# An RWKV-7 scan with a SwiGLU block on one core: the copies of chunks 6 to 23 go from VectorE to ScalarE, in a new order of steps

## The chip, the cores and the metric

The kernel runs on one core of one Trainium2 chip. The metric is the time of one execution in device microseconds (us); of several runs the median counts. In the profile PE is TensorE (PEld its weight loads), DVE VectorE, ACT ScalarE, POOL GpSimd and SP the sync engine, which here only issues DMAs.

## The reference, cut to what matters

```
# attention: batch 4, heads 8, sequence 768, head_dim 40
for t in range(S):
    y[:, :, t] = einsum('bhd,bhde->bhe', rt, state)
    Sa = einsum('bhde,bhe->bhd', state, at)
    state_decay = state * wt[:, :, None, :] - einsum('bhd,bhe->bhde', Sa, bt)
    state = state_decay + einsum('bhd,bhe->bhde', vt, kt)
# then x = y as (3072 tokens, 320), d_ff = 1536
xn = x / sqrt(mean(x * x, -1) + 1e-6) * rms_g
g = xn @ w_gate
out = (g * sigmoid(g) * (xn @ w_val)) @ w_out
```

The 32 pairs of batch and head each carry a 40 x 40 state through 768 steps. Their outputs, eight heads side by side, are the 3072 tokens of the feed-forward block. All is in fp32; the three weight matrices arrive as 64-bit floats and are narrowed on the chip.

## The kernel before, in words

The sequence is cut into 24 chunks of 32 steps. A chunk is solved as a small triangular system, so that the state is only touched once a chunk. There are five stages, each of them a function that adds steps to a plan:

- `narrow(f, part)`, 24 times: loads one half of a slice of the weights, turns its 64-bit words into fp32 with three ACT and three DVE steps, and writes it to a DRAM buffer `sW`.
- `front(c)`, one a chunk: loads w, a, k, b and v (tiles `wan`, `kbn`, `VU`, `wn`), turns them on PE, and builds by levels of 1, 2, 4, 8 and 16 the decay products `T`, the scaled keys `K`, the matrices `Ab` and `aP`, the keys `KN` and the triangular matrix `LT`, which goes by DRAM (`sB`) into `M`.
- `inverse(c)` (`early_inverse` for chunks 0 to 3): inverts that matrix row by row on DVE, with one product (`tmp`) and one difference (`Yi`, or `M` in the early form) a row, and sends it by DRAM (`sY`) back into `LT`.
- `main(c)`, one a chunk: computes U on PE from the old state, copies it into `VU`, updates the state `ST`, forms the scores, multiplies them into five masked tiles `As`, gets the output `y` level by level, and turns y into tokens: the sum of squares on ACT, a power on POOL, the scaling `x`, and its transpose scaled by the norm's weights (`gcol`) into `xg`.
- `feed(g)`, one for two chunks: for each pair of the twelve weight slices the gate and value products (`h64` and `h`, into PSUM), `sg` = silu on ACT, `hT` = value times `sg` on DVE, and the output product into `po` (line 547, as all of `mm`).

Each step goes through a helper with a line of its own, so the profile shows the helper's line: L505 for all DVE steps, L525 `act`, L528 `copy` and L531 `scale` on ACT, L534 to L540 POOL, L544 DMAs, L547 `mm`, L550 `flip` (a transpose), and L1079 the warm matmul.

No loop sets the order of the work. `plan.issue(ORDER, PAIRS)` walks through a list of some 6000 words written into the file: each number picks one of the steps not yet issued, counted from the first that is left, and each engine runs its own steps in the order in which they come. A "-" issues a warm matmul of `ident` by `ident` into columns of PSUM that nobody reads. `PAIRS` says which of three pairs of PSUM banks each of the 499 temporary PSUM tiles ("rooms") takes. A step may wait for the step before it on its engine, for its inputs, and for the earlier user of its PSUM pair or of its buffer, of which there are one to three for each tile.

Two constants choose forms by chunk: `EARLY` (4) the form of the inverse, `LATE` (6) the engine of four kinds of step in `main`:

```
for i, q in each_iq:                                              # line 892, four copies of U a chunk
    (copy if c < LATE else dcopy if q else copy)(VU[...], U[...])
for i in range(2):                                                # line 912, even chunks
    (copy if c < LATE else dcopy)(R["r2"][half(i)], ps[half(1 - i), i])
if G == 1 and c < LATE:                                           # line 929, the top mask
    for i in range(2):
        scale(As[:, j, :, i], sc..., msi[:, j, i, 0:1])
elif G == 1 or l == 1:
    tt(As[:, j], sc..., msi[:, j:j + 1]..., MUL)
if c < LATE:                                                      # line 997, the norm's weights
    for kt in range(KT): scale(xt[:, :, kt], ps[:, :, kt], gcol[:, kt:kt + 1])
else:
    tt(xt, ps, gcol..., MUL)
```

`copy` and `scale` are ACT steps, `dcopy` and `tt` DVE steps. `KT` is 3. In `each_iq` half of the four entries have q = 1.

Of the kernel before, what the change touches and what calls it, by code (L numbers as in the profile page):

```python
# [22 lines left out]
EARLY, LATE = 4, 6  # L23
# [10 lines left out]
4 5 6 7 8 9 10 11 - - 46 - - - - 43 53 18 - 316 323 58 - - 61 47 60 525 27 44 - - - - 12 13 14 15 16 17 19 317  # L34
- - 313 315 324 314 333 327 328 - 318 325 - 326 - - 73 339 - 74 85 93 84 - 94 82 83 334 337 - 336 335 338 -
340 349 20 21 22 350 355 23 342 343 24 25 26 - 367 - 354 348 - 352 - 344 345 363 346 365 347 - - 351 75 76 362
353 360 628 397 29 - 443 455 - 452 442 36 32 56 - 48 38 59 54 31 441 35 456 - 636 - 451 444 - 62 453 446 33 -
454 - 37 70 45 - 626 445 - 41 638 356 125 122 - 1 332 331 321 103 322 113 114 329 - 95 86 98 379 359 78 79 364
87 361 374 366 - 376 - 378 - - - - 373 77 357 368 371 377 375 387 372 89 88 358 - 461 - 386 369 383 90 80 -
380 381 465 370 466 384 - - 99 463 464 462 470 341 - 91 471 - - 478 - - 481 482 - 385 467 395 468 477 - - 476  # L40
- 483 493 480 - 389 391 390 - - 104 392 81 394 393 105 123 102 472 490 479 627 633 64 42 50 398 448 34 - 623 -
57 67 624 55 - 459 49 634 460 449 52 65 457 51 635 637 - - 473 - 474 491 - 475 450 - - 625 96 492 - 97 396 494
- - 489 - 504 382 100 487 488 - 484 506 - - 399 400 495 401 - 402 403 503 404 - - - 485 496 405 406 407 500
408 409 - 410 505 - 411 - 412 413 414 415 416 507 417 418 497 419 516 420 421 643 422 423 424 - 499 425 426
427 428 - 106 644 - - 502 501 498 107 108 429 124 320 0 317 90 576 - 132 577 - 328 99 643 645 511 510 - 484 -
113 646 644 509 107 - - - - 506 - 507 - 512 658 - 386 650 651 - 663 467 675 - - - 108 116 - 109 662 428 647
516 517 518 515 131 - 521 114 648 124 522 - 657 508 - - - 652 429 578 567 524 - - 61 870 456 861 860 - 640 66
445 430 69 - 598 871 26 - 28 64 639 630 67 629 110 519 520 434 656 - 653 - 654 661 - 117 660 659 127 128 - 655
580 - 115 - - 674 - - 579 513 664 - - - 432 143 431 433 118 525 526 670 568 125 126 669 133 581 666 134 135
435 436 437 438 569 141 142 140 119 687 129 - 668 673 667 161 152 151 163 - 665 144 527 528 529 136 137 138  # L50
679 530 531 532 533 671 534 535 536 537 147 676 160 130 573 571 572 570 672 682 145 146 684 148 538 680 539
540 541 542 543 544 545 546 547 548 149 549 550 685 551 552 553 - 554 582 583 686 - 574 153 555 575 681 156
677 162 139 801 164 678 586 688 167 157 689 - 589 595 590 - 604 693 154 165 155 690 587 588 596 1 0 962 135
145 144 113 146 134 663 519 661 662 560 136 137 143 612 121 122 660 556 557 555 646 554 712 520 664 665 562
129 138 655 147 148 149 563 131 564 568 565 132 569 - 713 566 832 668 33 - 827 841 826 825 - - 837 521 - 835
669 842 828 836 838 0 830 524 522 523 165 521 164 714 656 658 569 138 653 713 669 670 671 - 672 570 673 149
674 571 - 572 675 676 677 678 525 842 526 847 846 843 845 844 - 848 527 153 154 132 162 665 528 715 163 962
139 679 680 150 140 174 141 681 151 682 859 683 684 685 851 849 858 666 852 863 686 687 688 853 717 719 716
718 155 166 156 857 861 689 854 864 690 855 158 691 860 159 856 169 876 157 - 160 850 862 - 692 - 869 722 720
723 - - 546 764 182 - 152 183 185 173 167 547 726 573 168 875 574 - 721 - 575 729 731 865 1009 1008 - 600 -  # L60
1019 599 1018 1016 576 866 693 888 730 735 867 738 737 694 734 732 193 161 184 577 657 175 727 578 728 736 874
695 696 697 868 698 699 871 - 870 739 186 963 733 170 171 - 966 964 - 176 965 177 - 187 873 188 746 745 178
179 740 952 741 742 743 744 - 877 883 879 882 700 194 - - 579 881 880 747 180 872 887 886 172 195 885 580 748
582 - 878 889 891 581 884 749 750 751 752 753 829 590 589 1010 1020 896 754 892 - 890 1026 1013 1027 205 701
202 203 1021 1012 - 1022 - 1023 702 828 1028 705 703 950 951 755 - - 1011 894 893 838 756 1017 0 725 726 576
15 851 850 577 848 772 16 852 849 855 864 17 714 8 - 9 10 18 856 857 578 580 867 - 869 581 525 1093 579 19 23
33 719 720 32 853 723 854 868 862 863 877 866 879 523 717 0 573 515 575 516 713 869 517 847 707 710 711 574 42
0 509 5 839 840 845 841 707 861 567 753 850 14 754 855 856 755 893 568 708 709 569 570 757 853 710 - 711 8 17
851 712 713 714 715 716 717 718 854 719 871 523 21 23 22 867 852 858 756 - 872 - 766 868 524 - 866 869 873 720
# [4 lines left out]
776 876 877 878 18 879 880 881 882 883 884 885 748 - - 871 749 872 - - 1073 944 945 1078 1077 1075 1076 1074  # L74
23 560 719 561 1079 720 562 563 5 6 7 1082 1083 8 - 1090 886 887 1095 1093 1106 1080 947 564 0 12 715 24 - 712
556 13 16 1080 714 23 713 0 878 879 880 0 0 1072 875 1068 709 550 1069 1075 1070 876 1078 1087 877 710 10 1085
11 18 0 1073 1081 1080 9 875 1068 548 549 - - 708 - 1077 709 - 1085 1083 1079 - 929 758 759 876 1086 0 926
1077 17 1087 549 550 22 992 0 15 14 1193 12 542 543 544 765 1239 764 1250 1033 775 1043 867 868 869 1052 750
870 1090 871 872 1082 751 1240 920 1085 752 923 1089 1099 873 1083 874 875 876 1088 9 877 878 879 922 1084 921
545 1079 926 546 880 881 882 0 1085 1079 15 5 18 926 882 0 15 16 5 1079 545 546 1089 928 - 547 - - 548 - - -  # L80
939 1090 882 883 884 8 885 886 887 888 889 890 930 1093 1085 751 1091 929 1094 941 549 551 550 552 937 935 936
18 931 1092 19 891 932 553 938 940 892 893 894 895 896 897 933 898 899 900 942 554 555 1099 1098 1100 9 1101
972 - 0 1170 1083 1084 1085 0 196 546 - 0 0 385 343 344 551 - 386 - 345 552 376 346 - - 387 349 347 415 348
350 354 353 352 351 364 365 390 - 196 195 548 388 549 197 389 553 - 537 554 555 556 557 558 559 560 561 562
563 391 392 393 394 395 - 564 565 566 567 568 569 570 571 572 573 574 575 576 577 396 273 634 637 636 635 0 0
0 0 - 617 393 394 - 0 0 0 615 691 676 463 675 686 680 690 674 687 682 685 684 677 474 571 572 573 574 575 392
576 577 578 579 580 581 582 583 584 585 586 587 588 589 590 591 592 593 464 393 394 395 617 361 362 692 698
396 695 694 - 696 697 693 - - - 398 397 399 758 701 702 712 - 618 400 401 402 616 709 714 594 595 596 597 699
# [1023 lines left out]
```

## Time and profile before

| | |
|---|---|
| median of 3 runs | 1048.17 us (1045.47 to 1050.28) |
| span of the profiled execution | 1035.9 us |
| time around that span | not given by the page; median less span is 12.3 us |
| busy PE / DVE / ACT / POOL | 989.6 / 832.1 / 450.8 / 309.1 us |
| warm matmuls (L1079) | 522 records, 92.5 us of PE |
| chain that ended last | PE 54%, DVE 30%, issue 5%, DMA 5%, ACT 3% |

A group's row names line, engine, operation, output and input tile, shapes and count, then busy us and mean ns of one, then the idle time of the engine just before and what ended it. A row of the stretches gives from and to, the length, then for PE, PEld, DVE, ACT and POOL the busy us and the number of instructions, then the granted TensorE clock, the DMA share and GB/s. A row of the chain gives start, length and work. One warm matmul makes two records, as each fp32 matmul here does.

### The profile page before, as it was taken

How to read it: one execution, taken by the hardware profiler on the slowest of the kernel's cores; microseconds unless marked ns; L12 is line 12 of the kernel's file. 1: busy time of each engine (PE TensorE's matmuls, PEld its weight loads, DVE VectorE, ACT ScalarE, POOL GpSimd, SP SyncE). 2: the span in 40 equal slices, each digit the busy share in tenths (PEclk: the TensorE clock that was granted, in tenths of full speed). 3: DMA queues.
4: the chain of work that ended last, by engine and by line, in shares of the span. 5: the costliest groups of instructions: out<-in, count | busy, mean ns of one | idle time of the engine just before them, and what ended most of it. 6: DMA issues, size and time to landing. Idle time of an engine off the chain costs nothing.

```text
span 1035.9 us, 56007 instructions
## 1 busy us (share of the span) xinstructions
PE 989.6 (96%) x24842; PEld 807.6 (78%) x24842; DVE 832.1 (80%) x2789; ACT 450.8 (44%) x1019; POOL 309.1 (30%) x554
## 2 busy tenths in 40 slices
PE   7987999999999999999999999999999999999998
PEld 7976877788887787787877787887787877778876
DVE  8987688686869899899989888888799898788410
ACT  5784775543553443443443433452434444341210
POOL 9633413041442233232244232333232432210000
PEclk9976699999999999999999999998999999999999
DMA  8877356755442634434443535334633624422222
GB/s 161 158 194 171 97 158 165 202 131 127 105 87 64 145 79 103 120 65 106 101 98 83 143 75 125 87 68 99 133 62 68 162 65 107 114 51 54 89 77 65
DMA packets 163538, 113.03 MB, mean 109 GB/s; under 512 B 124512, under 2 KB 142880, under 8 KB 163296
## 3 DMA queue, kind: packets, MB, share of 16 engines
q1 hardware_dynamic: 144928, 86.48, 33.8%
q0 software_dynamic: 16192, 22.64, 11.3%
q8 instruction: 195, 3.19, 1.3%
q10 hardware_dynamic: 2176, 0.33, 0.3%
q14 instruction: 47, 0.39, 0.1%
HBM read 93.39 MB, written 15.99 MB: 106 GB/s over the span
## 4 chain that ended last, share of the span: by engine, by line
PE 54%; DVE 30%; issue 5%; DMA 5%; ACT 3%; SPq 2%; POOL 1%; DVEq 0%; ACTq 0%; POOLq 0%
PE ps L547 36%; PE po L547 10%; DVE tmp L505 5%; DVE Yi L505 5%; PE ps L550 5%; DVE LT L505 4%; PE po L1079 3%; DVE K L505 3%; DVE As L505 2%; SPq L544 2%; DVE Ab L505 1%; DVE hT L505 1%; DMA wf<-sW 1%; DVE y L505 1%; DVE T L505 1%
## 5 line engine op out<-in xcount | busy, mean ns | idle before, releaser
L547 PE MATMUL ps<-xg,wf 128*128 128x256 f32 (+1 forms) x1728 | 353.8, 391 | 1.1 <-DMA wf<-sW 0.7
L547 PEld LDWEIGHTS ps<-xg,wf 128*128 128x128 f32 (+1 forms) x1728 | 263.1, 190 | 50.6 <-issue 15.2
L547 PE MATMUL po<-wf,hT 128*128 128x320 f32 x576 | 177.0, 445 | 0.1
L505 DVE TENSOR_TENSOR tmp<-Yi,M 128x60 f32<-128x60 f32 (+24 forms) x620 | 130.3, 210 | 19.8 <-DMA M<-sB 5.4
L505 DVE TENSOR_TENSOR Yi<-Yi,tmp 128x60 f32<-128x60 f32 (+24 forms) x620 | 129.8, 209 | 14.6
L525 ACT ACTIVATE sg<-ps 128x512 f32<-128x512 f32 x72 | 43.0, 597 | 216.5 <-PE ps L547 216.3
L547 PEld LDWEIGHTS po<-wf,hT 128*128 128x128 f32 x576 | 104.6, 191 | 37.0 <-issue 2.1
L544 POOL DMA_DIRECT2D kbn<-in_b_dram x92 | 53.8, 587 | 191.7 <-PE ps L547 169.9
L528 ACT COPY KN<-ps 128x640 f32<-128x640 f32 x96 | 66.3, 692 | 88.0 <-DVE LT L505 50.5
L505 DVE TENSOR_TENSOR K<-K,T 128x512 f32<-128x512 f32 (+1 forms) x192 | 94.0, 496 | 3.4 <-ACT K L528 2.7
L1079 PE MATMUL po<-ident 128*128 128x128 f32 x522 | 92.5, 313 | 3.3 <-DVE po L579 3.3
L505 DVE TENSOR_TENSOR hT<-ps,sg 128x512 f32<-128x512 f32 x72 | 49.6, 689 | 51.6 <-ACT sg L525 51.0
L528 ACT COPY K<-K 128x256 f32<-128x256 f32 (+1 forms) x168 | 72.6, 444 | 35.2 <-DVE K L505 25.0
L547 PEld LDWEIGHTS ps<-Ab,K 40*60 40x60 f32 (+2 forms) x4608 | 68.7, 129 | 19.7 <-issue 6.5
L505 DVE TENSOR_TENSOR As<-ps,msi 128x256 f32<-128x256 f32 (+1 forms) x186 | 82.9, 478 | 1.1 <-PE ps L547 0.6
L547 PE MATMUL ps<-Ab,K 40*60 40x56 f32 (+2 forms) x4608 | 78.2, 217 | 5.2 <-DVE K L505 2.5
L1079 PEld LDWEIGHTS po<-ident 128*128 128x128 f32 x522 | 73.9, 208 | 11.5 <-POOL wan L540 3.3
L544 POOL DMA_DIRECT2D VU<-in_v_dram x92 | 53.8, 586 | 93.5 <-PE ps L550 55.9
L547 PEld LDWEIGHTS ps<-As,KN 128*40 128x40 f32 x3072 | 68.1, 128 | 13.9 <-issue 8.4
L544 POOL DMA_DIRECT2D wn<-in_w_dram x92 | 51.9, 566 | 90.0 <-DVE KN L505 56.4
L547 PE MATMUL ps<-As,KN 128*40 128x32 f32 x3072 | 74.0, 208 | 3.7 <-issue 1.5
L544 POOL DMA_DIRECT2D kbn<-in_k_dram x92 | 53.4, 583 | 76.7 <-PE ps L547 73.3
(137 smaller groups left out, 1470.3 us busy)
## 6 DMA issues: line engine op xcount, KB each, us to landing
wf<-sW SPq DMA_DIRECT2D x82, 480.0 KB, 4.4
M<-sB SPq DMA_DIRECT2D x80, 128.0 KB, 3.6
rn<-in_r_dram SPq DMA_DIRECT2D x24, 160.0 KB, 5.0
out_dram<-o SPq DMA_DIRECT2D x48, 80.0 KB, 3.2
kbn<-in_b_dram POOLq DMA_DIRECT2D x92, 40.0 KB, 3.1
kbn<-in_k_dram POOLq DMA_DIRECT2D x92, 40.0 KB, 3.2
wan<-in_a_dram POOLq DMA_DIRECT2D x46, 80.0 KB, 3.7
wan<-in_w_dram POOLq DMA_DIRECT2D x46, 80.0 KB, 4.3
```

Of the source, the lines that this page charges most:

```text
L505: plan.add("DVE", kind, lambda at: fn(at(o), *m(at)), [o], aps(*args))
L525: plan.add("ACT", "act", lambda at: nc.scalar.activation(at(o), at(a), f, **kw), [o] + aps(acc), [a])
L528: plan.add("ACT", "copy", lambda at: nc.scalar.copy(at(o), at(a)), [o], [a])
L544: plan.add(by, "dma", lambda at: queue.dma_start(out=o, in_=i), [o], [i])
L547: return o, lhsT, rhs, lambda at: nc.tensor.matmul(at(o), lhsT, rhs, start=start, stop=stop, skip_group_check=True)
L550: return o, i, ident, lambda at: nc.tensor.transpose(at(o), i, ident)
L1079: plan.warm = lambda: nc.tensor.matmul(po_[:, 0, DM:DM + P], ident, ident, start=False, stop=False, skip_group_check=True)
```

## The change

`LATE` becomes 24, so all 24 chunks take the branch that chunks 0 to 5 took: in chunks 6 to 23 ACT makes all four copies of U instead of two, the two half copies of r in even chunks, the top mask as two scalings instead of one DVE product, and the norm's scaling as three scalings instead of one DVE product. The numbers of `ORDER` and `PAIRS` are new throughout; the old list has 6131 words with 261 "-", the new one 5949 with 25. Nothing else differs.

```diff
-EARLY, LATE = 4, 6
+EARLY, LATE = 4, 24
...
 ORDER = """
-4 5 6 7 8 9 10 11 - - 46 - - - - 43 53 18 - 316 323 58 - - 61 47 60 525 27 44 - - - - 12 13 14 15 16 17 19 317
...
+4 325 314 5 6 44 317 7 323 8 69 328 9 324 43 10 313 11 58 12 83 13 454 73 45 627 74 445 85 47 94 456 93 628 113 397
+333 318 458 326 337 14 15 16 334 18 75 350 355 367 48 17 441 316 338 19 637 20 78 327 76 336 23 335 442 315 114 27
...
```

More of the change, by code (lines that the diff above doesn't have):

```diff
@@ L39 @@
[L39 to L68, printed above, removed]
@@ L78 @@
[L78 to L87, printed above, removed]
@@ L208 @@
-573 574 638 562 217 417 418 703 699 694 692 704 702 695 705 693 709 494 419 - 420 732 575 576 577 578 579 731
-744 - 0 0 216 - 561 419 420 421 422 740 716 578 579 754 714 646 715 647 430 719 431 432 723 580 649 648 724
[34 rows of a table removed]
-574 575 576 577 578 579 580 581 582 583 584 585 - 586 587 588 589 590 591 592 593 594 433 595 596 597 638 598
[8 rows of a table removed]
[5 rows of a table added]
+368 636 386 107 384 461 383 108 398 369 385 462 91 380 465 370 623 464 463 109 92 54 381 390 634 391 638 392 - 68
[3 rows of a table added]
+408 - 484 502 65 28 492 506 42 70 49 803 500 582 600 525 409 487 153 52 41 132 32 504 410 411 66 72 165 499 412 413
[7 rows of a table added]
@@ new lines @@
+686 203 549 550 693 551 552 553 588 554 176 555 677 688 595 628 678 556 174 604 - - 175 689 590 699 177 698 592 863
+697 594 593 864 700 591 0 836 552 520 550 828 147 560 838 653 150 835 141 156 664 600 559 665 0 0 373 414 689 375 0
+414 373 676 415 416 0 415 23 0 372 690 560 416 449 561 498 494 563 5 6 502 417 - 15 0 417 372 517 15 22 6 418 518
+696 7 31 0 511 411 25 8 0 688 411 689 23 511 8 512 495 681 513 412 514 684 21 413 414 683 364 365 0 677 506 507 508
+0 672 675 508 356 4 357 856 0 844 508 374 854 4 21 6 509 510 22 5 404 405 30 543 0 838 297 0 503 838 23 671 504 0
@@ new lines @@
+504 366 535 538 671 505 678 506 484 683 536 507 537 0 667 27 0 822 27 535 17 18 670 502 503 0 503 670 1 2 - 0 817
+501 502 503 504 505 532 663 - 506 507 4 508 509 0 534 663 474 545 31 521 0 382 680 532 28 660 531 664 383 384 665
[3 rows of a table added]
+741 17 493 30 0 664 0 543 666 542 541 0 0 658 607 665 23 815 666 807 808 657 32 14 685 - 544 671 809 668 811 669 6
+1053 672 810 670 546 24 15 674 545 812 824 829 486 547 0 809 480 2 15 541 810 666 735 10 670 821 9 11 0 803 734 733
+831 539 540 735 478 721 0 828 667 478 803 8 492 493 669 668 671 675 670 676 722 842 724 677 678 679 680 681 - 682
[6 rows of a table added]
@@ new lines @@
+540 840 1047 1055 766 700 0 0 1052 537 837 840 697 1036 15 1048 913 914 841 1237 - 1049 538 916 539 1050 843 844
[7 rows of a table added]
+484 640 331 332 333 334 529 541 335 0 334 335 336 337 338 339 471 340 341 342 369 0 - 1110 342 343 344 537 551 369
+621 552 635 622 388 715 345 346 347 349 553 636 348 392 393 - 554 394 624 194 197 350 555 395 196 699 195 396 556
[37 rows of a table added]
+389 678 666 958 0 436 - 660 971 959 - 969 960 769 608 609 775 774 662 777 659 437 961 668 958 661 970 432 438 610
[24 rows of a table added]
+869 881 826 870 880 876 1173 868 827 702 861 456 464 862 828 873 871 877 467 872 691 874 964 - 692 694 882 883 829
[6 rows of a table added]
@@ new lines @@
+771 596 597 598 599 642 644 600 744 601 602 643 756 - 959 437 741 745 757 436 603 640 604 605 606 755 1 740 761 556
+749 760 758 - 754 977 - 645 607 1127 608 646 751 752 763 609 610 764 753 - 774 611 612 772 766 433 765 613 438 655
+439 614 615 389 616 617 618 619 620 621 647 656 659 390 670 775 622 623 968 773 672 449 1126 778 434 777 440 769
+759 776 666 767 663 - 648 441 779 713 497 442 660 662 661 459 855 624 625 626 958 668 458 667 665 671 703 664 679
[3 rows of a table added]
+451 452 985 993 989 636 994 857 861 997 860 859 996 858 - 1174 453 1173 807 808 809 810 990 811 864 454 865 1007
[13 rows of a table added]
@@ new lines @@
+672 459 - 673 759 770 - 661 660 762 771 769 855 631 713 458 671 669 674 675 676 677 678 679 963 1 962 680 960 783
+784 681 977 785 786 787 447 767 973 788 633 853 452 448 766 854 789 682 454 634 790 791 792 793 794 795 683 970 856
+796 684 636 797 685 798 455 799 800 801 802 803 804 805 961 978 983 972 806 780 979 982 971 980 987 807 981 988 781
+808 809 456 986 810 811 812 813 814 - 984 985 815 686 687 688 816 817 999 460 818 461 637 635 1182 994 689 690 989
[35 rows of a table added]
+1028 873 871 1026 468 685 686 830 872 687 688 689 1190 875 876 469 690 0 414 718 0 409 405 568 574 - 416 564 403
[29 rows of a table added]
@@ L253 @@
 """
 PAIRS = """
-01201021021121101111100201222022221011011000100001122202211122111122100202212212021112100022210101002021100100
-00211011112122201012221112110222022101002022021022000022112002221200021110010002020012000022101112110211102211
-01212202001212120012221101012120220002010011000201100020112112122201102001011101101022222222112121010200020022
-11212211201222001100100021021212220112210110100222011010000020111202122210000011120021120221122002000210000212
-00211111002010002112212110121110100201010121000220212012012
+0120102012102020221001202211011121011202020212222100200201111100220220211101021010112221010111122221021120010002022
@@ L261 @@
+2212220020000101101002122121010222010212021012112111201022111010022021010020001211220212002221202222121102221001112
+0100102101022001012020222011202022002100122020201111220101212121021200002100021012212121122001220210111211120211212
+2020011122001012210112222011101001200012002022120222212221000101111020202110112201221220100222020002212112101210110
+120221001000020201012110011001221212102
 """
```

69 lines of the change are left out of this document (removed), and 282 rows, old and new, of the table ORDER.

## The prediction

> **What bounds the kernel now.** I read the page from its top (engine shares, slices, chain), then the stretches of the span, then the groups behind the moved steps, then the chain near the start.
>
> ```profile
> span 1035.9 us, 56007 instructions
> PE 989.6 (96%) x24842; PEld 807.6 (78%) x24842; DVE 832.1 (80%) x2789; ACT 450.8 (44%) x1019; POOL 309.1 (30%) x554
> ...
> PEclk9976699999999999999999999998999999999999
> ...
> PE 54%; DVE 30%; issue 5%; DMA 5%; ACT 3%; SPq 2%; POOL 1%; DVEq 0%; ACTq 0%; POOLq 0%
> ```
>
> PE is busy nearly all the time, DVE 80%, ACT not half. The chain that ended last is 54% PE and 30% DVE: two engines in turn, PE the harder limit. The busy share of PE holds filler, though: the warm matmuls of line 1079, which compute nothing. So I set them against the whole in five stretches; first all work, then that line alone.
>
> ```profile
> core 0: us, PE busy (x) PEld busy (x) DVE busy (x) ACT busy (x) POOL busy (x), PEclk, DMA share, GB/s
> 0.00:52.00 52.00, 46.50 (x1016) 43.29 (x1017) 47.70 (x137) 33.22 (x72) 40.77 (x91) 1.00 0.82 159
> 52.00:130.00 78.00, 65.00 (x1983) 58.10 (x1981) 57.61 (x174) 53.05 (x116) 29.24 (x57) 0.69 0.62 154
> 130.00:208.00 78.00, 71.70 (x1925) 57.84 (x1925) 62.03 (x196) 47.55 (x102) 15.56 (x27) 0.98 0.68 177
> 208.00:936.00 728.00, 711.29 (x18548) 574.73 (x18552) 629.84 (x2189) 300.93 (x700) 222.43 (x379) 1.00 0.43 98
> 936.00:1036.00 100.00, 95.10 (x1390) 73.62 (x1384) 34.92 (x96) 16.04 (x32) 1.10 (x2) 1.00 0.25 73
> ```
>
> ```profile
> core 0: us, PE busy (x) PEld busy (x), PEclk, DMA share, GB/s
> 0.00:52.00 52.00, 32.24 (x232) 29.22 (x233) 1.00 0.82 159
> 52.00:130.00 78.00, 22.38 (x105) 17.48 (x103) 0.69 0.62 154
> ...
> 208.00:936.00 728.00, 29.64 (x142) 20.72 (x142) 1.00 0.43 98
> ```
>
> In the long stretch from 208 to 936 us, which holds most of chunks 6 to 23, PE does 711.29 - 29.64 = 681.7 us of real work in 728: 46.3 us are filler or idle. That is all that better feeding can win there. DVE stands at 629.8 of 728. In the first 52 us DVE is at 92% (47.70 of 52) and PE does only 46.50 - 32.24 = 14.3 us of real work; from 52 to 130 us it does 65.00 - 22.38 = 42.6 us, at a granted clock of 0.69. The last 100 us are feed matmuls alone, 95.1 us of them; nothing in the change touches these.
>
> **Part 1: the moved steps.** `LATE` goes from 6 to 24, so chunks 6 to 23 (18 chunks, nine of them even) take the ACT branch everywhere. Four kinds of step move; here are the DVE groups they come from and the ACT groups of chunks 0 to 5 that show their price.
>
> ```profile
> L505 DVE COPY VU<-ps 32x320 f32<-32x320 f32 x36 | 17.3, 480 | 6.9 <-ACT VU L528 6.2 <-PE ps L547 0.2
> L505 DVE COPY r<-ps 64x512 f32<-64x512 f32 x18 | 12.4, 689 | 2.6 <-PE ps L550 1.5 <-ACT rE L528 0.7
> L505 DVE TENSOR_TENSOR As<-ps,msi 128x512 f32<-128x512 f32 x42 | 28.5, 684 | 0.0
> L505 DVE TENSOR_TENSOR xg<-ps,gcol 128x384 f32<-128x384 f32 x18 | 9.9, 556 | 6.6 <-PE ps L550 6.6
> L528 ACT COPY VU<-ps 32x320 f32<-32x320 f32 x60 | 25.0, 417 | 23.1 <-PE ps L547 11.7 <-DVE VU L505 10.4
> L528 ACT COPY r<-ps 64x512 f32<-64x512 f32 x6 | 3.5, 580 | 2.5 <-PE ps L550 2.4
> L531 ACT ACTIVATE As<-ps,msi 128x256 f32<-128x256 f32 x12 | 5.5, 471 | 7.2 <-DVE As L505 4.8 <-PE ps L547 2.4
> L531 ACT ACTIVATE xg<-ps,gcol 128x128 f32<-128x128 f32 x18 | 5.7, 387 | 3.9 <-PE ps L550 3.8
> ```
>
> Off DVE: 36 U copies x 0.480 = 17.3; 18 r copies x 0.689 = 12.4; the top mask, 18 of the 42 wide As products (the other 24 are the level-1 mask, one a chunk) x 0.684 = 12.3; 18 scalings x 0.556 = 10.0. Sum 52.0 us, DVE from 832 to 780. Onto ACT: 36 x 0.417 = 15.0; 18 x 0.580 = 10.4; 36 half masks x 0.471 = 17.0; 54 thirds of the scaling x 0.387 = 20.9. Sum 63.3 us, ACT from 451 to 514, half of the span. The list of steps agrees: one piece for three in the scaling and one for two in the mask make 18 x 3 = 54 more steps, and the new order holds 5924 against 5870.
>
> What that is worth, two ways. By the chain: DVE's 30% of 1035.9 is 310.8 us, 37% of its 832.1 busy, so 52.0 x 0.37 = 19.4 us would leave the chain; ACT's 3% is 31 us, 7% of 450.8, so 63.3 x 0.07 = 4.4 would enter. Net -15. By the slack of PE: DVE sheds 52.0 of 629.8, 8.3%, and if the 46.3 us that PE wastes shrink alike, the gain is 4: what is next late when a DVE stall goes is PE itself. I take -10, about the middle; the ends are -19 and 0.
>
> **Part 2: the order.** Each engine works through its steps in the list's order. Numbering the steps as the code adds them and following both lists, I compared how tight they are: for each PE step from the 160th on, how many PE steps lie between it and the last PE step its inputs need, by way of every queue and PSUM room. At most one lies there in 20 cases before and 26 after, exactly two in 155 and 157. The new list gives PE about the same distance to cover its inputs; I see no reason in it for a gain or a loss and take 0. The SP and POOL queues are rearranged too: the page's chain gives SPq 2% and DMA 5%. The last weight step stands at place 1283, warm marks not counted, in both lists, and no DMA is added. I take 0 there, within 10 us either way: SPq's 2% is 21 us, and half of it could go or come.
>
> **Part 3: the warm matmuls.** The old list has 261 marks "-", the new one 25; up to the last weight step 190 against 10. So the start loses nearly all its filler. What that filler does is seen in the chain:
>
> ```profile
> 3.31 5.69 PE po L1079 x30
> 19.16 1.10 PE ps L547 x64
> ...
> 105.07 1.86 PE ps L547 x64
> ```
> ```profile
> by line: PE ps L547 23.4%; issue 9.4%; PE po L1079 9.3%; DVE LT L505 4.6%; PE ps L550 4.6%; DVE K L505 4.3%; PE po L547 4.2%; DVE wf L505 3.2%; DMA wf<-sW 2.6%; DVE tmp L505 2.6%; DVE M L505 2.5%; DVE Ab L505 2.2%; ACT KN L528 2.0%; DMA wf<
> ```
> ```profile
> 104.00:120.00 16.00, 15.87 (x346) 14.03 (x345) 11.41 (x34) 9.82 (x22) 3.10 (x6) 0.50 0.38 104
> ```
>
> A batch of 64 small matmuls takes 1.10 us where the clock is full and 1.86 where it is 0.50, 1.7 times as long; and from 104 to 120 us the clock stays at 0.50 though PE shows 15.87 of 16 us busy. So small matmuls alone do not raise the clock, and without filler I expect 0.5 from the start until the feeds begin. Cost: 14.3 x 0.7 = 10.0 us in the first stretch. From 52 to 130 us a clock of 0.69 means full speed in 0.38 of the time (0.38 x 1 + 0.62 x 0.5): 42.6 x 0.38 x 0.7 = 11.3. Together 21 us of PE time, if all lies on the path. Real PE work is 23.4 + 4.6 + 4.2 = 32% of the chain of 0 to 208 us (second fence), so I take 7 on the path. Gain: filler is 9.3% of that chain, 19 us, time in which a real batch stood behind it. In the first 52 us DVE has no room to use it; in the rest I count 7 back, about the share that 22.38 us of 54.62 has in the 19 (7.8). The start comes to 0, with ends -19 and +21.
>
> The Trainium skill, page "TensorE: Matmul & The Clock Gate", section "Why this matters for your kernels", says to leave no idle gaps over about 3 us between matmul bursts, or the clock halves; the 15.87 busy us at 0.50 show that here even gap-free small batches do not keep it. By that rule the start would pay the +21, rival C.
>
> **Sum.** -10 + 0 + 0 on a span of 1035.9 gives 1025.9. The median of the three runs is 1048.17; the page gives no time around the span, so I carry the difference of 12.3: 1038. The forecast's own range, relief between -5 and -19 and up to 3 us from the start, is 1026 to 1043.
>
> **Rivals.**
> A, the forecast: DVE's relief shows in the long stretch, the start evens out. 1038, chance 0.50.
> B, hidden anyway: PE's 681.7 us of real work bind, and the freed DVE time only becomes DVE idle time. For it: PE is at 98% in the long stretch; against: DVE's 30% of the chain. 1048, chance 0.18.
> C, slower, a cold start: the whole +21 is paid and nothing comes back from the filler, with the relief as above: 1035.9 - 10 + 21 + 12.3 = 1059. It decides once the start costs over 10 us more than it gives back. For it: 190 marks become 10; against: DVE, at 92%, hides PE there. Chance 0.16.
> D, slower, ACT in series: U's four copies shared by two engines took the longer of 2 x 0.417 and 2 x 0.480, 0.96 us, and take 4 x 0.417 = 1.67 on one: +0.71; the mask 0.94 for 0.684: +0.26; the scaling 1.16 for 0.556: +0.60; r, behind rE's copy
>
> ```profile
> L528 ACT COPY rE<-ps 128x1024 f32<-128x1024 f32 x12 | 12.1, 1012 | 16.5 <-PE ps L547 8.4 <-PE ps L550 7.5 <-DVE r L505 0.4
> L525 ACT ACTIVATE sg<-ps 128x512 f32<-128x512 f32 x72 | 43.0, 597 | 216.5 <-PE ps L547 216.3
> ```
>
> on the same engine, 1.01 + 1.16 for 1.38, +0.79 in every second chunk, 0.40 a chunk. Together 1.97 x 18 = 35 us if each ended the path; half of it, without the relief, gives 1035.9 + 18 + 12.3 = 1066. It decides where over 10 of the 35 us fall on the path. ACT also runs in order: the silu steps wait 216.3 us for PE, and in the new list 18 of the 36 half masks and 19 of the 54 scalings stand behind an ACT step that needs later PE work. Against it: two chunks of lead and ACT at half load. Chance 0.16.
> The Trainium skill, page "ScalarE: Activation LUTs", section "Rules for kernel authors", advises VectorE and not ScalarE for a plain mul; the rows agree for the scaling (1.16 against 0.556) and disagree for the U copy (0.417 against 0.480). By it D would be likelier.
> That the change does not do what it says is ruled out by the count of steps.
>
> **How the numbers follow.** About 0.5% is what a measurement of this kernel can tell: 5.2 us, so "same" is 1043 to 1053. A is faster, 0.50; B same, 0.18; C and D slower, 0.32. The range runs from the full relief with a start that gives back 13 of the 19 us of filler on its chain, 1035.9 - 19 - 13 + 12.3 = 1016, to D at half price, 1066. Less than 2 in 10 is left out: the full 35 of D, or a far better order.
>
> **What would show it.** Right: DVE busy near 780 and ACT near 514; from 208 to 936 less than 46 us of filler and idle time on PE; DVE's share of the chain below 30%; granted clock about 0.5 up to the first feed matmul, and that one within 10 us of where it starts now, 132.2 us:
>
> ```profile
> L547 PE MATMUL ps<-xg,wf x1728: 376/379/792, 132.2 to 1026.0; 128*128 128x256 f32 x120, 64*128 64x256 f32 x72
> ```
>
> Wrong: a first feed later by 15 us or more (C); ACT over 6% of the chain, with PE waiting for U, As or xg (D); or PE's idle time unchanged while DVE's grows (B).

## The result, and the profile after

| | before | after |
|---|---|---|
| median, in one comparison | 1049.22 us (1045.47 to 1052.47) | 1058.01 us (1053.84 to 1063.67) |
| span of the profiled execution | 1035.9 us | 1053.5 us |

The ratio is 1.010 with an interval of 1.0067 to 1.0134: slower by 1%, where 1038 was forecast. The medians lie 8.8 us apart and the two profiled spans 17.6, because the profiled execution of before was a short one: it took some 1038 us, by the 1.8 us that the other executions of before take beyond their spans, and the four in the table took 1045 to 1052. So about half of the 17.6 us may be a difference between executions. The page of the changed kernel, in the lines shown of before, and its queue of instructions:

```profile
span 1053.5 us, 55159 instructions
...
PE 948.2 (90%) x24370; PEld 770.8 (73%) x24370; DVE 794.7 (75%) x2699; ACT 505.2 (48%) x1163; POOL 310.6 (29%) x554
...
PEclk9997689799999999999999999999999899999999
...
q8 instruction: 191, 3.13, 1.3%
...
PE 72%; DVE 10%; DMA 7%; issue 6%; SPq 2%; ACT 2%; POOL 1%; DVEq 0%; ACTq 0%
```

DVE's part of the chain has gone from 30% to 10%, as the forecast said it would; PE has risen from 54% to 72%, and the whole is longer. The same five stretches show where PE stands still:

```profile
core 0: us, PE busy (x) PEld busy (x) DVE busy (x) ACT busy (x) POOL busy (x), PEclk, DMA share, GB/s
0.00:52.00 52.00, 23.16 (x628) 20.62 (x628) 43.08 (x122) 32.95 (x68) 41.37 (x89) 1.00 0.92 194
52.00:130.00 78.00, 55.23 (x1952) 50.22 (x1952) 65.62 (x198) 53.66 (x115) 29.93 (x56) 0.80 0.68 162
130.00:208.00 78.00, 65.64 (x1769) 52.83 (x1764) 50.16 (x152) 41.93 (x93) 17.52 (x31) 0.87 0.55 136
208.00:953.00 745.00, 708.77 (x18619) 572.22 (x18619) 604.74 (x2149) 354.21 (x840) 220.63 (x376) 0.99 0.43 97
953.00:1053.00 100.00, 95.42 (x1409) 74.92 (x1408) 31.16 (x82) 22.42 (x49) 1.11 (x2) 0.99 0.25 73
```

The clock of 1.00 in the first row, and in part the 0.80 of the second, isn't a measured clock: the trace of after has its first record of the clock at 89.2 us, that of before at 7.7 us. The same batch of 64 matmuls, at the start of after and then of before, shows the clock:

```profile
23.52 1.85 PE L533 MATMUL ps<-Ab,K 40*60 40x56 f32 x64
```
```profile
19.16 1.10 PE L547 MATMUL ps<-Ab,K 40*60 40x56 f32 x64 [1.97 <-DVE K L505]
```

1.85 us is the time that before has for it at a clock of 0.50 (1.86), so PE runs the start of after at about half its clock, as was forecast.

The feed matmuls begin as before, at 132.1 us. Then the two part: the first copy of an output `o` starts at 232.3 us before and at 251.4 after, and from there to the end of the span it is 803.6 us before and 802.1 after. The rows are those of the tiles `xg` and `o`, of after, then of before:

```profile
L533 PE MATMUL ps<-xg,wf x1728: 373/379/795, 132.1 to 1043.4; 128*128 128x256 f32 x120, 64*128 64x256 f32 x72
L514 ACT COPY o<-po x12: 677/692/701, 251.4 to 1048.1; 128x640 f32<-128x640 f32 x12
```
```profile
L528 ACT COPY o<-po x12: 679/692/712, 232.3 to 1030.8; 128x640 f32<-128x640 f32 x12
```

So in this pair of profiles the 17.6 us of the span are lost between the first feed matmul and the first output. What PE waited for there, in the waits of after from 125 to 251 us, then of before from 125 to 232 (total, times, longest):

```profile
PE ps L533 <- issue: 17.3, 9, 4.1
```
```profile
PE ps L547 <- issue: 3.2, 4, 1.3
```

"issue" is a wait for nothing that the profile shows. The chain of after in that stretch names its pieces, and the longest one can be looked into:

```profile
146.55 3.41 issue
...
186.29 3.50 issue
...
230.45 4.11 issue
```
```profile
229.65 0.69 PEld L533 LDWEIGHTS ps<-As,KN 128*40 128x40 f32 x32
229.65 0.80 PE L533 MATMUL ps<-As,KN 128*40 128x32 f32 x31
...
234.56 0.21 PE L533 MATMUL ps<-As,KN 128*40 128x32 f32 x1 [4.11 <-issue]
```
```profile
226.45:230.45 4.00, 3.63 (x179) 2.80 (x178) 3.33 (x18) 3.19 (x6) 0.16 (x1) 1.00 1.02 245
230.45:234.56 4.11, 0.00 (x0) 0.00 (x0) 0.00 (x0) 0.27 (x1) 0.00 (x0) 0.76 0.64 83
234.56:238.56 4.00, 4.00 (x34) 3.61 (x34) 3.48 (x15) 1.96 (x6) 0.65 (x1) 0.50 0.24 38
```

The second fence is the timeline: a batch of 32 matmuls on the same two tiles stops after 31, and the last one comes 4.11 us later. Its inputs were there, its weights had been loaded with the other 31. The third fence is the stretches before, in and behind the stop: all engines stand, the DMA engines had been full (1.02), and behind it the clock is 0.50. The DMA view of 230.4 to 234.6 us shows one packet of the queue "instruction":

```profile
q1 hardware_dynamic: 2075, 0.33, 60.9%
q8 instruction: 1, 0.02, 2.5%
```

In the records this packet of 16 KB lies from 231.5 to 233.2 us, and PE goes on 1.35 us after its end. I call such a stop, over 0.7 us between two matmuls of one batch with no semaphore in between, a **break**, and counted them: 9 with 15.3 us before, 22 with 39.6 us after; between 125 and 235 us 1.3 and 18.1 us, which is nearly the 19 us by which the first output is late. Three counts say that PE waits for its own program. The queue moves 191 packets of 16 KB, and 2 x 24370 PE instructions in blocks of 256 make 190.4; before, 195 against 194.1. Every break of these two kernels ends 1.2 to 2.0 us after such a packet lands. And they lie at one slowly drifting place of the block: numbered from PE's first instruction, modulo 256, all breaks around 165 us are at 134 in after and in two kernels below that have 64 and 224 more instructions ahead of it. A batch that was slow by its data would have moved by those 64 or 224.

The Trainium skill, page "Runtime: NRT & Kernel Launch", section "Instruction fetch mechanics", says the same of how the code comes: an engine's instructions are refilled in blocks of 16 KiB, 256 instructions, by a DMA queue of its own. It adds that crossing a block is "mostly hidden"; in after that holds for most of the 191 blocks, but at least 22 were not hidden, for 39.6 us.

### The profile page after: what moved, and what is told of

It reads as the page before. It is cut to its first block, busy times and chain, and to the rows that moved or that the text cites. A ratio compares the mean times of both kernels' runs of the same rounds, so it can differ in the third digit from the quotient of the medians.

```text
span 1053.5 us, 55159 instructions
## 1 busy us (share of the span) xinstructions
PE 948.2 (90%) x24370; PEld 770.8 (73%) x24370; DVE 794.7 (75%) x2699; ACT 505.2 (48%) x1163; POOL 310.6 (29%) x554
## 4 chain that ended last, share of the span: by engine, by line
PE 72%; DVE 10%; DMA 7%; issue 6%; SPq 2%; ACT 2%; POOL 1%; DVEq 0%; ACTq 0%
PE ps L533 52%; PE po L533 13%; PE ps L536 7%; SPq L530 2%; DVE LT L491 2%; DMA kbn<-in_k_dram 1%; DVE y L491 1%; DVE tmp L491 1%; DMA sY<-Yi 1%; DMA M<-sB 1%; DVE K L491 1%; DVE wf L491 1%; DVE Yi L491 1%; DVE As L491 1%; DMA LT<-sY 1%
## 5 line engine op out<-in xcount | busy, mean ns | idle before, releaser
L533 PE MATMUL ps<-xg,wf 128*128 128x256 f32 (+1 forms) x1728 | 363.1, 399 | 7.2 <-issue 6.5
L533 PEld LDWEIGHTS ps<-xg,wf 128*128 128x128 f32 (+1 forms) x1728 | 270.2, 194 | 56.4 <-issue 20.6
L533 PE MATMUL po<-wf,hT 128*128 128x320 f32 x576 | 180.2, 450 | 4.5 <-DVE hT L491 2.3
L491 DVE TENSOR_TENSOR Yi<-Yi,tmp 128x60 f32<-128x60 f32 (+24 forms) x620 | 130.7, 211 | 15.5
L533 PE MATMUL ps<-Ab,K 40*60 40x56 f32 (+2 forms) x4608 | 82.5, 226 | 16.4 <-DVE K L491 6.5
L533 PEld LDWEIGHTS ps<-Ab,K 40*60 40x60 f32 (+2 forms) x4608 | 73.8, 137 | 31.4 <-issue 17.5
L491 DVE TENSOR_TENSOR As<-ps,msi 128x256 f32<-128x256 f32 (+1 forms) x168 | 69.9, 456 | 16.0 <-PE ps L533 8.8
L491 DVE TENSOR_TENSOR y<-y,ps 128x256 f32<-128x256 f32 x119 | 49.9, 419 | 23.8 <-PE ps L533 20.7
L520 POOL TENSOR_TENSOR ss<-ss,mhalf 128x1 f32<-128x1 f32 x24 | 14.5, 606 | 150.4 <-DVE ss L491 146.6
```

The source lines that it names most:

```text
L491: plan.add("DVE", kind, lambda at: fn(at(o), *m(at)), [o], aps(*args))
L520: plan.add("POOL", "tt", lambda at: nc.gpsimd.tensor_tensor(o, a, b, op), [o], [a, b])
L533: return o, lhsT, rhs, lambda at: nc.tensor.matmul(at(o), lhsT, rhs, start=start, stop=stop, skip_group_check=True)
```

## The experiments

All ratios are to the kernel before in the same comparison. In the lists, "-" is a start matmul (a warm matmul: two matmuls and two loads, four instructions).

**Which half of the change: steps or order.** First the moved steps alone, each in ACT's queue where it ran on DVE before:

```diff
-EARLY, LATE = 4, 6
+EARLY, LATE = 4, 24
```
with the old list and all 261 "-" kept (the list is 54 words longer for the steps that become several).

> LATE is 24 in the old order: the moved steps alone. Each takes the place among ScalarE's steps that the start of its VectorE step in the trace of before gives it; all 261 warm marks stay. Order theory (the new list arranges the stretch from the first feed to the first output, 132 to 250 us, worse): same as before, 1049 within 5 us. Clock theory (the missing warm marks leave TensorE at half clock): same, 1049 within 5. Moved-steps theory (the ScalarE series costs what VectorE's relief gives, and more): 1058 or more. The prediction's relief of 10: 1039.

Measured 1059.83 us, 1.0138 (1.0102 to 1.0175). PE's instructions are the old ones, its breaks too (10 with 15.5 us). DVE is relieved and falls to 13% of the chain, ACT rises to 5%:

```profile
PE 1004.1 (95%) x24842; PEld 819.2 (77%) x24842; DVE 787.3 (74%) x2699; ACT 502.6 (47%) x1163; POOL 309.6 (29%) x554
...
PE 68%; DVE 13%; ACT 5%; issue 5%; DMA 4%; SPq 3%; POOL 1%; DVEq 0%; ACTq 0%; POOLq 0%
```

The first output is 3 us late, the sixth 7, the tenth 25. So in a list that was not made for them the moved steps cost 1.4%, 14 us (24 us of span against the short profile of before); in number this is near rival D. Between 545 and 883 us PE waited 3 us for ACT's `y`, `Sd` and `xg`, 11.7 for "issue" (before, 541 to 859: 0.3 for ACT, 8.1 for "issue"). These do not make up the whole. Of the 24 us of span 14.5 are PE's own busy time (1004.1 us against 989.6, for the same 24842 matmuls), at a mean clock of 0.956 against 0.972; why the clock was lower stays open.

Then the other half, the new list with `LATE` at 6:

```diff
-EARLY, LATE = 4, 24
+EARLY, LATE = 4, 6
```

> LATE is 6 in the new order with its 25 marks: the moved steps undone, each VectorE step placed by the start of its ScalarE steps in the trace of after. Order theory: 1058 within 5. Clock theory: 1058 within 5. Moved-steps theory: 1049 or less. The prediction's relief of 10: 1068.

Measured 1092.56 us, 1.044 (1.0394 to 1.0485), DVE with 24% of the chain, 20 breaks with 31.9 us. None of the theories on record comes near it (1049 to 1068). It has fewer breaks than after and is 3.4% longer, with DVE back in the chain: in this list the moved steps are worth some 35 us. The old list with the steps moved isn't told apart from both together (1.0138 and 1.0100, their intervals overlap). List and steps belong together, and neither half alone explains the loss.

**The start matmuls.** The old list without its 190 "-" up to the last weight step:

```diff
-4 5 6 7 8 9 10 11 - - 46 - - - - 43 53 18 - 316 323 58
+4 5 6 7 8 9 10 11 46 43 53 18 316 323 58
```

> The kernel before with its 190 warm marks up to the last weight step left out, nothing else. Order theory: 1049 within 5. Clock theory: about 1049 + 17 = 1066, the clock at 0.5 to 130 us and at times until 250 us. Prediction's step on the start: 1049, between 1030 and 1070.

Measured 1055.78 us, 1.0107 (1.0064 to 1.0149), between the 1049 of the order theory and the 1066 of the clock theory. In the profile, which is of the shortest execution (1045.58), the first feed matmul stands at 132.4 us for 132.2, the first output is 10 us late and nothing is added behind it, and 10.3 of 29.4 us of breaks lie between 130 and 250 us. The first batches of 64 small matmuls there start one every 23 to 25 ns, where before starts them every 13 to 14: half the clock in the start didn't delay the first feed. The other way round, 158 "-" put into the new list up to 250 us, as many as fill PE's idle time (the first place of them):

```diff
-113 397 333 318
+113 397 - - - - - - - - - - - - - - - - - - - - - - 333 318
```

> The kernel after with 158 warm marks more, put ahead of the TensorE steps up to 250 us in proportion to the engine's idle time before each in the trace of after. Order theory: 1058 within 5, the first output still at about 251 us. Clock theory: 1041 to 1045, with a full clock from the start and the first output at about 235 us.

Measured 1100.19 us, 1.0534 (1.0487 to 1.0581), 41 breaks with 66.4 us. The clock theory asked for a first output at 235 us and 1041 to 1045 in all; the first output came at 253.8 and the whole is 42 us slower than after. It isn't a clean trial of a full clock, for the clock stayed at 0.73 from 30 to 130 us, and the 158 "-" also shift all that follows by 632 instructions. At this point only one thing went along with the times, the breaks.

**The place in the block.** "-" ahead of PE's first step shift all that follows. 16 of them are 64 instructions, a quarter of a block:

```diff
-... 113 397 333 318
+... 113 397 - - - - - - - - - - - - - - - - 333 318
```

> The kernel after with 16 warm marks more ahead of TensorE's first step, where the engine is idle for 6.6 us anyway: no step changes place, but all later TensorE instructions come 64 further along their stream. Code theory (TensorE waits in the middle of a batch for the next 16 KB of its instructions, 39.6 us in all after against 15.3 before): these waits fall on other batches, and the span follows their sum, about 1014 + sum, anywhere from 1035 to 1075. Order theory and clock theory: same as after, 1058 within 5.

> The kernel after with 16 marks more ahead of TensorE's first step and 32 ahead of its second, both in idle stretches (6.6 and 11.6 us): the stream is shifted by 192 instructions. Code theory: again another sum of waits in mid-batch, span about 1014 + sum, between 1035 and 1075 and not the same as with 16 marks. Order theory and clock theory: 1058 within 5.

(the second with 32 more ahead of PE's second step). Measured 1099.82 us, 1.0513 (1.0464 to 1.0562), and 1055.06 us, 1.0116 (1.0082 to 1.0151). The work is the same; a quarter of a block is worth 42 us, and the span of the first, 1097, is over the 1075 that the code theory had as its top. The old list was shifted the other way, by leaving out its first 15, 32 and 48 "-", and the new one brought to half a block; the first of these begins

```diff
-4 5 6 7 8 9 10 11 - - 46 - - - - 43 53 18 - 316 323 58 - - 61 47 60 525 27 44 - - - - 12
+4 5 6 7 8 9 10 11 46 43 53 18 316 323 58 61 47 60 525 27 44 12
```

> The kernel before without its first 15 warm marks, ahead of TensorE's first step: no step changes place, the TensorE stream is 60 instructions shorter at its head. Code theory: mid-batch waits move, their sum is another than 15.3, and the span goes with it, up to 40 us longer. Order and clock theories: same as before within 5.

> The kernel before without its first 32 warm marks (up to 13 us): the stream is 128 instructions shorter. Code theory: again another sum of mid-batch waits, span 1030 to 1080. Order theory: same as before within 5. Clock theory: 1 to 3 us slower.

> The kernel before without its first 48 start matmuls: 192 instructions of TensorE fewer, three quarters of a block of 256. With minus 15 and minus 32 this makes four places in the block a quarter apart (0, -15, -32, -48), as with 0, +16, +32 and +48 of the new list. Place theory: the old list's own place is a lucky one, so this one lies between 1055 and 1105 us like the two others (1077 and 1102). Rival, the old list is short at nearly every place and the two others were the odd ones: 1040 to 1052.

> The kernel after with 16 start matmuls ahead of TensorE's first step and 16 ahead of its second: 128 instructions, half a block. The new list has 1058 at 0, 1100 at +16 and 1055 at +48. Place theory: anywhere between 1040 and 1100, and the four places of the new list have a mean that is at most that of the old one's four (the relief of some 9 us lies within the scatter). Rival, the new list is slower at every place: over 1060 here, and its mean of four above that of the old list.

The four places of each list, the last row an eighth more:

| kernel, "-" more or fewer | ratio (interval) | span | breaks | first output to end |
|---|---|---|---|---|
| before | 1 | 1035.9 | 15.3 | 804 |
| before, -15 | 1.0329 (1.0287 to 1.0370) | 1075.3 | 38.4 | 837 |
| before, -32 | 1.0531 (1.0483 to 1.0578) | 1101.0 | 47.2 | 854 |
| before, -48 | 1.0345 (1.0284 to 1.0407) | 1074.4 | 33.9 | 834 |
| after | 1.0100 (1.0067 to 1.0134) | 1053.5 | 39.6 | 802 |
| after, +16 | 1.0513 (1.0464 to 1.0562) | 1097.1 | 60.9 | 850 |
| after, +32 | 1.0349 (1.0273 to 1.0425) | 1074.7 | 50.8 | 829 |
| after, +48 | 1.0116 (1.0082 to 1.0151) | 1053.5 | 34.1 | 808 |
| after, +56 | 0.9975 (0.9936 to 1.0014) | 1039.0 | 26.0 | 797 |

The mean of the four quarters is 1.030 for the old list and 1.027 for the new one: no difference that these runs can tell. The order and the clock theory, which asked for no change within some 5 us at these places, fall. The old list without its first 32 "-" is over the range of the code theory, too (a span of 1101 where 1080 was the top). Breaks, spans and the last column are from one profile each, and that of before is a short one. The old list stands at its best place of the four, and the change moved the program to another. Behind the first output, where a list of one kind does the very same steps, the place alone moves the time between 797 and 850 us, and PE's waits for "issue" with it. From the first output on, after, then the same with 16 "-":

```profile
PE ps L533 <- issue: 16.0, 16, 3.2
PE ps L536 <- issue: 2.3, 3, 1.0
PE po L533 <- issue: 2.2, 2, 1.7
```
```profile
PE ps L544 <- issue: 41.9, 36, 4.2
PE ps L547 <- issue: 6.0, 5, 2.1
PE po L544 <- issue: 2.2, 2, 1.1
```

20.5 us against 50.1: 30 of the 48 us are the waits themselves; the clock of that stretch falls from 0.99 to 0.96, so PE's busy time grows too, from 768 to 793 us. The last row of the table was run to see whether the new list has a good place:

> The kernel after with 16 start matmuls ahead of TensorE's first step and 40 ahead of its second: 224 instructions, one eighth of a block ahead of its own place, between the two better places found so far (0 at 1058, +48 at 1055). Place theory: 1040 to 1065, and under 1046 if the good stretch of places has its middle here. Rival, the new list's best is its own 1055 to 1058 and it never comes under the old list's 1047: 1053 to 1065.

It has: 1041.38 us against 1042.61, not told apart. The whole loss of the change is made good by 56 start matmuls that compute nothing, and no version that loads all its weights beats the kernel before.

**Old start, new rest, and the other way round.** The old list up to the first output's copy with the new one behind it (`LATE` 24), and the new list up to there with the old one behind it (`LATE` 6). The joints, each against the kernel that it starts as:

```diff
-531 723 708 0 618 603 712 723 710 604
+531 723 708 0 416 680 699 941 942 952
...
-619 401 0 2 622 731 726 402
+619 401 0 581 582 583 584 585
```

> The old list up to the first output's copy (232 us before), the new list from there, LATE 24. Start theory (the whole loss arises ahead of the first output): 1058 - 19 = 1039. Moved-steps theory (the loss is in the ScalarE series): 1058. Code theory: span about 1014 + sum of the mid-batch waits, with few of them ahead of 232 us.

> The new list up to the first output's copy, the old list from there, LATE 6: no step moved. Start theory: 1048 + 19 = 1067. Moved-steps theory: 1048. Code theory: the waits of after ahead of 251 us (18 us from 125 us on) stay, those behind it are new.

Measured 1054.32 us, 1.0073 (1.0032 to 1.0114), and 1060.53 us, 1.0153 (1.0101 to 1.0206). The second has no moved step at all and loses at least as much as the change did; in its profile the first output is 14.6 us late and the others are 20 to 23:

```profile
L524 ACT COPY o<-po x12: 685/692/712, 246.9 to 1053.4; 128x640 f32<-128x640 f32 x12
```

Its breaks of 3.3 and 3.4 us stand at 143 and 180 us, as those of after at 147 and 186. The first has its first output at 232.7 us and loses 13 later, by breaks again (20 with 30.8 us); so the theory that the whole loss arises ahead of the first output, which asked for 1039, falls. Shifted by leaving out the last 16 and 32 "-" ahead of the joint, it gets worse (one of the places):

```diff
-1098 1100 9 1101 972 - 0 1170
+1098 1100 9 1101 972 0 1170
```

> The old list up to the first output's copy and the new list behind it (1054), without the last 16 start matmuls ahead of the joint: 64 instructions fewer in all that follows, the start of the old list nearly unchanged. Place theory: first output within 5 us of 233, and the stretch behind it, 816 us at the old place with 20 stalls in all, moves by 10 to 40 us either way. Rival, the new list's rest is 12 us longer than the old one's whatever its place: 1050 to 1058.

> The same joint without the last 32 start matmuls: 128 instructions fewer. Place theory: the stretch behind the first output moves by 10 to 40 us against 816, in either direction; if it falls to about 790, as with the small weight loads less their saving, the whole comes to 1030 and beats both kernels. Rival, the rest of the new list is 12 us longer whatever its place: 1050 to 1058.

Measured 1060.31 us, 1.0151 (1.0084 to 1.0217), and 1085.0 us, 1.0357 (1.0294 to 1.0420): from the first output to the end 816 us becomes 822 and 843, the breaks 34.0 and 43.6 us. The first moved by 6 us only, less than the 10 expected; the rival of a fixed 12 us falls with the second.

**Less data beside the code.** If the code is late because data fill the DMA engines, thinner loads must bring it sooner. The repeated loads of weight tiles were cut to a quarter (76 of 82, 120 KB for 480):

```diff
-                    dma(wf, sW[f + e])
+                    cut = WF // 4 if wf.tensor.name in loaded else WF
+                    loaded.add(wf.tensor.name)
+                    dma(wf[:, 0:cut], sW[f + e][:, 0:cut])
```

> The kernel after, but 76 of the 82 loads of narrowed weights bring only a quarter of their columns (120 KB for 480 KB; each of the six tiles is loaded in full once): the same instructions, less traffic beside the loading of code, and wrong weights in most products. Code theory (blocks of instructions queue behind the data): the mid-batch waits fall from 39.6 us to about 20, the first output from 251 us to about 240, the span to about 1030. Order theory: the first output stays 15 us or more behind that of g2.

> The kernel before with the same cut of 76 loads, which leaves the weights of most products wrong. Code theory: mid-batch waits from 15.3 to about 10 us, span about 1028, so that g1 and g2 lie within 8 us. Order theory: g1 stays 17 us behind, as after does behind before.

Measured 1016.38 us, 0.974 (0.9691 to 0.9788), and 1025.57 us, 0.9812 (0.9761 to 0.9864). By the ratios the cut is worth 3.6% (some 38 us) to the new list, whose breaks fall from 39.6 to 20.4 us, and 1.9% (20 us) to the old one, whose breaks hardly move (14.0, where 10 were expected). With it the new list is the shorter one by 9.2 us in the medians, but the two intervals overlap. The waits from its first output on, beside those of after above:

```profile
PE ps L533 <- issue: 4.4, 7, 1.5
PE ps L536 <- DMA wan<-in_w_dram: 1.3, 1, 1.3
```

The last run took the same cut to the worst place of the new list:

> The kernel after at its worst place (16 start matmuls ahead of TensorE's first step, 1100 us) with the second and later loads of each weight tile cut to a quarter (120 KB of 480), as in the run that brought the new list at its own place from 1058 to 1016; all else is computed, from weights that are three quarters stale. Place theory, TensorE's code waits behind the data: most of the 42 us between the two places goes with the traffic, 1016 to 1035, and in-batch stalls fall from 60.9 us to under 30. Rival, the bad place costs by itself (the 16 matmuls, the clock, the order of the first steps): it stays some 42 us above 1016, at 1050 to 1062.

Measured 1049.37 us, 1.0074 (1.0028 to 1.0120), breaks 40.7 us. By the ratios it is 46 us less than with full loads, but 35 more than the same cut at the new list's own place: this expectation missed, and the rival's 1050 was the nearer number. So the weight loads lengthen the waits for code, by about 20 us of breaks at either place of the new list, but they are not what makes a place good or bad. Here the rest from the first output on still waits 23.9 us:

```profile
PE ps L544 <- issue: 23.9, 23, 2.4
```

What makes a place bad can be read from the records, though no run changed it alone. The border of a block is known where it broke and interpolated in between, so these figures are estimates. In after the packet of a block starts 1.2 us (median) behind PE's entry into the block before it, and 3.1 us behind it where a break follows; it takes 1.1 us, and at a break PE goes on 1.2 to 2.0 us after its end. So the code comes one block ahead and no more, and a break needs a packet that starts late or a block that PE runs through quickly. Thin loads make late starts rarer: packets that start over 2.5 us behind the entry are 28 in after and 9 with the cut, 30 and 19 at the worst place. The place decides on quick blocks, by how many blocks of 256 instructions hold small matmuls alone (no feed or warm matmul of 128 x 128): 15, 37, 41, 33 and 19 in the new list at 0, +16, +32, +48 and +56, and 9, 23, 24 and 20 in the old one at 0, -15, -32 and -48. Blocks that PE runs through in under 3 us are 10 in after, 32 at +16, and still 27 there with thin loads.

## Why the prediction was wrong

**The step that failed** is Part 2, "I see no reason in it for a gain or a loss and take 0". Both lists were compared by the distance of PE's steps to their inputs. The time that PE needs to get its own program was no term of the sum, though the page of before has the queue and its chain 5% "issue". In the two profiles it measured 18.1 us of breaks against 1.3 between 125 and 235 us, where the first output came 19 us late, and by place the rest moves by up to 53 us (797 to 850; 804 to 854 for the old list). With the forecast's own -10 those 19 us give +9, and the medians are 8.8 apart; as the profile of before is a short one, that this comes out so closely is partly luck. A new list is a new place for every batch, and no sum over steps gives it.

Nearly all the signs that were to show the forecast right came: DVE's share of the chain at 10%, PE's filler and idle time below 46 us, a start at about half the clock, the first feed matmul at 132.1 us, ACT near 514 (505.2); only DVE's busy time stayed above its 780. None of them looked at the stretch between the first feed and the first output, or at PE's waits for "issue".

**Part 1, the relief, holds in mechanism.** The groups that were to leave DVE left it: 17.3 + 12.4 + 9.9 us of U, r and scaling, and the wide masks are

```profile
L491 DVE TENSOR_TENSOR As<-ps,msi 128x512 f32<-128x512 f32 x24 | 16.4, 684 | 1.0 <-ACT As L517 1.0
L514 ACT COPY VU<-ps 32x320 f32<-32x320 f32 x96 | 40.1, 417 | 24.7 <-PE ps L533 22.2 <-DVE Yi L491 1.1
L517 ACT ACTIVATE xg<-ps,gcol 128x128 f32<-128x128 f32 x72 | 22.5, 370 | 22.9 <-PE ps L536 20.4 <-DVE y L491 2.5
```

16.4 us instead of 28.5, together 51.7 for the 52.0 of the sum. But DVE's busy line fell by 37.4 only, to 794.7 and not 780. The line counts overlapping records once: the records of DVE add up to 963.8 us before, against 832.1 on the page. ACT rose by 54.4 for 63.3. The time it was to bring, 10 us, is not shown by itself. With thin loads the new list is 9.2 us shorter, but the intervals overlap and each list has a place of its own. At full loads pairs with like breaks say 21 (before -15 with 38.4 us of breaks has a span of 1075.3, after with 39.6 has 1053.5; before -48 with 33.9 has 1074.4, after +48 with 34.1 has 1053.5); that is an estimate from single profiles, and it holds the 20 us of filler that the new list has left out behind the first output (24.81 us against 5.03). The plainest sign of the relief is the new list with `LATE` 6, 3.4% longer with fewer breaks. The new list gives the relief back in breaks: 46 us in the mean of its four quarters for 34. (The last 100 us of before were read as feed matmuls alone; 80.5 of the 95.1 us are, the rest is of the last chunks.)

**Part 3, the cold start, cost nothing up to the feeds.** The start has lost its filler and runs at about half the clock (1.85 us a batch for 1.10), PE's first stretch is down from 46.5 to 23.2 us of busy time, and still the first feed matmul stands at 132.1 us for 132.2: up to there the 0 of this part was right. Rival C gave 1059, the measured time, by a reason that did not act: its sign was a first feed later by 15 us, and it wasn't late. That its number fits is luck.

**Rival D** comes near in number in the old list (1059.83 with the moved steps alone for its 1066), but its sign does not: ACT has 5% of that chain, not over 6, and PE waits 3 us for it. In after ACT has 2%. **Rival B** asked for PE's idle time to stay while DVE's grows. From the first output on PE's filler and idle time is 46.2 us before (803.6 less 782.16 of busy time, and 24.81 of filler in it) and 38.8 after (802.1 less 768.37, and 5.03), from these rows of both, all work and then the warm matmuls alone:

```profile
232.30:1035.90 803.60, 782.16 (x19389) 628.28 (x19387) 643.24 (x2197) 305.76 (x704) 211.17 (x360) 1.00 0.41 94
...
232.30:1035.90 803.60, 24.81 (x112) 16.84 (x112) 1.00 0.41 94
```
```profile
251.40:1053.50 802.10, 768.37 (x19171) 618.50 (x19169) 604.31 (x2112) 356.31 (x839) 210.09 (x358) 0.99 0.41 94
...
251.40:1053.50 802.10, 5.03 (x26) 4.06 (x26) 0.99 0.41 94
```

DVE has 39 us less to do in it and PE wastes 7 us less; the work of PE itself took 6 us longer, at a clock of 0.99 for 1.00. So the long stretch gains 1.5 us where 10 were forecast.

**The 12.3 us around the span** were for the most part a difference between executions, not a constant: the profiled execution of after took 1055.42 us with a span of 1053.5, 1.9 us around it. The other 10 us came from a short execution having been profiled; adding them turned a forecast for that execution into one for the median.

## What to carry to other kernels

Where a kernel is one long straight program and TensorE is busy over 90% of the time, look first for "issue" among its waits and for stops inside a batch, and compare their ends with the packets of the instruction queue. Before a new order is judged, shift its program by a quarter of a block or two and compare means: one list at one place tells nothing below some 5% here. Moved steps are tried with the list made for them: the new list without them was 3.4% slower than with them.

## What the runs showed of the hardware

PE can stand for up to 5.1 us in the middle of a batch (the old list with thin loads), and 64 more instructions ahead of it change the time of the whole by 42 us. A stop of 4.11 us left the clock at 0.50 for the next 4 us, so a break can cost more than its length: over the places of the new list, 60.9 less 26.0 us of breaks go with 58 us of span. PE's code came one block of 256 instructions ahead, by the estimate above, and at the worst place PE ran through 32 of them in under 3 us. A granted clock of 1.00 ahead of the first record of the clock (89.2 us in after) is no measurement: the batches there took as long as at 0.50.
